# Longformer attention with a split-weight FFN: the first batch planned without mutual exclusion of VectorE and GpSimd

## The chip, the core and the metric

One core of a Trainium2 chip runs the whole program. The metric is the device time of one execution in microseconds. Engines are named as in the profile: PE (TensorE), DVE (VectorE), ACT (ScalarE), POOL (GpSimd), SP (SyncE, which issues the DMA transfers here). Each engine runs its own instructions strictly in the order in which the program gives them; semaphores make one engine wait for another.

## What is computed

Eight batches of attention (8 heads, 512 local and 32 global positions, head size 64) are followed by a feed-forward network with a leaky ReLU of one slope per unit:

```python
mask = np.abs(pos[:, None] - pos[None, :]) <= 32
s_ll = np.where(mask, scale * q_l @ k_l.T, -1e9)
a_l = sm(np.concatenate([scale * q_l @ k_g.T, s_ll], axis=-1))
out_l = a_l @ np.concatenate([v_g, v_l])
out_g = sm(scale * q_g @ k_all.T) @ v_all
x = concat(out_g, out_l)              # 4608 x 512
h = x @ w_in                          # 512 -> 2048
g = np.maximum(h, 0) + alpha * np.minimum(h, 0)
y = g @ w_out                         # 2048 -> 512
```

The weights come as 64-bit floats and are decoded on the chip into two single-precision parts (an upper and a lower one); inputs of the two products are split in the same way, and three of the four partial products are added up.

## The kernel before

**Tiling.** A batch has four pairs of heads (P runs over all 32 pairs) and 16 blocks of 128 hidden units (t, or f within a batch). For each block PE forms h = x times w_in (12 matmuls, `f1`) into a PSUM bank, DVE and ACT make g from it, and PE adds g times w_out into four banks (8 matmuls `fa` with the upper part of g, 4 `fb` with the lower part `gl`). The attention of the next batch runs between these blocks.

**Batch 0 is different.** Before its first product there is attention of four pairs to do, and the weights have to be decoded while they are first used: 32 halves (k = 2f + j; j = 0 is w_in, j = 1 is w_out). One half takes the steps below. The names are those of the plan, with the number of the half behind them (d314 is d3 of half 14).

| step | engine | what |
|---|---|---|
| Lw | SP | load the raw words |
| cv, ab | ACT | low words to integers, absolute value of the high ones |
| d1, d2, d3 | DVE | clamp, shift (both TENSOR_SCALAR, wraw from wraw), sign (SCALAR_TENSOR_TENSOR, wt from wraw) |
| ia | POOL | add the rounding (TENSOR_TENSOR, wt from wt and wr) |
| ca | ACT | upper part |
| su | DVE | lower part (TENSOR_TENSOR, wt from wt) |

Other names that the prediction uses: S, T, V, G are PE's scores, transposes, value products and global scores of a pair; red, mn, rza, rzr are DVE's row maximum, its negation, the sum and its reciprocal, nm POOL's normalisation that rzr releases; gm, gz are the statistics of the global rows and gsc their normalisation (POOL for the first four pairs); tq, tr are DVE transposes; xl are lower parts of x; be makes beta from alpha; p makes g from PSUM, gh (ACT) and gl (DVE) are its two parts; yl are the lower parts of the x of batch 1 (yl0 to yl3, one for each pair).

**What sets the order.** The order in batch 0 is not that of loops. `early` lists some 690 operations with engine, cost in microseconds and needs; `Plan.run` schedules them: each engine has a time at which it is free, an operation can start when its needs are done, and among those that can start about now the one that is due first (`due_times`, shifted by a bias for each kind from the table `LIST`) is taken. The operations are issued in the order that comes out, and the engines of batch 0 keep it. In the version before, operations marked `lock=True` (nm and gsc of POOL, d1, d2, d3, su, yl and gl of DVE, ia of POOL and the making of the mask) never overlapped in the plan: `lock` is the time at which the last of them ended, and the next may not start earlier.

```python
if o["lock"]:
    t = max(t, lock)
...
free[e] = stop = t + cost
if o["lock"]:
    lock = stop
```

That holds in the plan only. On the chip nothing in the program keeps DVE and POOL apart; only the order in which their instructions stand was made with it.

**Behind batch 0.** From t = 16 on the order comes from loops: `slow_unit` for batch 1, whose DVE, ACT and POOL instructions a scheduler of the language may place earlier or later (PE's stay), and `fast_unit` from batch 2 on, which saves matmuls with sums of x and of weights. `weight_sums` (wsum on DVE, 8 groups of six operations) prepares these in batch 1.

Of the kernel before, what the change touches and what calls it, by code (L numbers as in the profile page):

```python
# [37 lines left out]
GOFF = 1024  # L38
GROWS = {1: (0, 0), 4: (0, 1), 7: (0, 2), 10: (1, 0), 13: (1, 1), 15: (1, 2)}
LIST = dict(  # L40
    first=29.416, pace=6.054, pair0=79.515, pair=19.51, slack=2, vsub=1, ahead=6, inflight=4, near=0.1, vgl=1, half=True,
    bias=dict(ab=14, rzr=20, red=-20, fb=10, mem=12, su=1, gm=-25, gsc=-3, rza=9, xA=-15, yh=-24, G=5, Tg=-8, yl=-8, pt=-6, n=2, Lw=16, Lv=-12, cv=5, al=15, T=-29, sr=-13, mk=-10, gz=-15, sq=-20, S=-4, fa=-6, V=4, fy=-15, gh=15, xg=-6, xlA=-15, hr=17, mn=-1, Lq=-1, tr=-2, f=-6, p=-1, gexp=-5, tq=-3, xlB=-1, clear=6, be=2, fx=3),
)
FAST = range(2 * NF, NB * NF)
CATCH = (16, 23, 30)
# [15 lines left out]
class Plan:  # L61
# [3 lines left out]
        self.slots = {k: [0.0] * n for k, n in slots.items()}  # L65
        self.ops, self.slack, self.near, self.bias = {}, slack, near, bias

    def op(self, name, engine, cost, needs=(), lock=False, take=(), free=(), kind=None, due=None, n=1):
        assert name not in self.ops, name
        self.ops[name] = dict(engine=engine, cost=cost, needs=[x for x in needs if x], lock=lock, take=take, free=free, kind=kind, due=due, n=n)  # L70

    def due_times(self):
        users = {n: [] for n in self.ops}
# [23 lines left out]
    def run(self):  # L97
        ops, users = self.ops, self.due_times()
        end, order = {}, []
        free = dict(PE=5.4, ACT=2.5, DVE=5.0, POOL=4.0, SP=1.2)  # L100
        lock, dma, kind, landed = 0.0, 3.3, None, [0.0] * 8
        left = {n: len(o["needs"]) for n, o in ops.items()}
        ready = {n for n, k in left.items() if k == 0}
        while ready:
            can = []
            for n in sorted(ready):
                o = ops[n]
                e = o["engine"]
                if any(len(self.slots[p]) < k for p, k in o["take"]):
                    continue  # L110
                t = free[e]
                for x in o["needs"]:
                    y = ops[x]["engine"]
                    lag = -100.0 if y == e == "SP" and n[0] != "h" else 0.3 if y == "PE" else 0.12
                    t = max(t, end[x] + lag)
                for p, k in o["take"]:
                    t = max(t, sorted(self.slots[p])[k - 1])
                if o["lock"]:
                    t = max(t, lock)
                if e == "SP":  # L120
                    t = max(t, landed[o["n"] - 9])
                can.append((t, o["at"], n))
            assert can, sorted(ready)
            t, _, n = min(can)
            e = ops[n]["engine"]
            t, _, n = min((c for c in can if ops[c[2]]["engine"] == e and c[0] <= t + self.near), key=lambda c: (c[1], c[0]))
            o = ops[n]
            cost = o["cost"]
            if e == "PE":
                cost = cost * (1.25 if t < 45 else 1.03) + (0.15 if kind != o["kind"] else 0.0)  # L130
                kind = o["kind"]
            if e == "SP":
# [24 lines left out]

def early(first, pace, pair0, pair, slack, vsub, ahead, inflight, near, vgl=0, half=False, bias={}):

    plan = Plan({"st": NST - 2, "w": NWB}, slack, near, bias)  # L160
    op = plan.op

    for P in range(9):
        pre = P < NRAW
# [6 lines left out]
        due = pair0 + pair * (P - 5) if P > 4 else None  # L171
# [11 lines left out]
        for h in range(2):  # L183
            old = [f"nm{P-2}.{e}" for e in range(2)] if P > 1 else []
            if not pre and h == 0:
                old.append(f"sq{P-1}" if P > NRAW else f"T{P-2}")
            op(f"red{P}.{h}", "DVE", 0.61 if pre else 0.86, [f"S{P}", f"red{P}.0" if h else None, None if pre else "mk0"] + old)
            if pre:
                op(f"mn{P}.{h}", "DVE", 0.07, [f"red{P}.{h}"])
            hold = h == 0 and pre  # L190
            op(f"ex{P}.{h}", "ACT", 1.5, [f"mn{P}.{h}" if pre else f"red{P}.{h}", f"ex{P}.0" if h else None, f"T{P-2}" if hold and P > 1 else None], take=(("w", 1),) if hold and P % 2 else ())
            op(f"rza{P}.{h}", "DVE" if pre else "ACT", 0.08 if pre else 0.13, [f"ex{P}.{h}"])
            op(f"rzr{P}.{h}", "DVE", 0.1, [f"rza{P}.{h}"])
            op(f"nm{P}.{h}", "POOL", 1.0, [f"rzr{P}.{h}"], lock=True)
# [6 lines left out]
        op(f"gexp{P}", "ACT", 0.52, [f"gm{P}", f"Tg{P-1}" if P else None])  # L201
        op(f"gz{P}", "DVE", 0.55, [f"gexp{P}"])
        if pre:
            op(f"gsc{P}", "POOL", 0.8, [f"gz{P}"], lock=True)
        else:
            op(f"gsc{P}", "ACT", 0.53, [f"gz{P}"])
        last = first + pace * 15.5 if P == 8 else None
        if not pre:
            op(f"tq{P}", "DVE", 1.23, [f"nm{P}.0", f"nm{P}.1"], due=last)
# [28 lines left out]
        if not pre:  # L238
            c = P - NPAIR
            op(f"yh{c}", "ACT", 0.53, [f"xA{P}", f"xB{P}"], take=(("st", 2),), due=first + pace * 15)  # L240
            op(f"yl{c}", "DVE", 0.61, [f"yh{c}"], lock=True, due=first + pace * 15.5)
    op("clear", "POOL", 0.18, [f"Tg{NGP-1}"])
    op("mk0", "POOL", 0.6, ["Tg0"], lock=True)
    op("al0", "SP", 0.3, ["Lq0"])
    op("be0", "DVE", 0.1, ["al0"])
    for P in (9, 10):
# [1 line left out]
    for k in range(2 * NF):  # L248
        f, j = divmod(k, 2)
        op(f"Lw{k}", "SP", 1.31, [f"d3{k-ahead}" if k >= ahead else None], take=(("w", 1),))  # L250
        op(f"cv{k}", "ACT", 0.66, [f"Lw{k}", f"su{k-inflight}" if k >= inflight else None], take=(("st", 1),))
        op(f"ab{k}", "ACT", 0.58, [f"cv{k}"])
        op(f"d1{k}", "DVE", 0.33, [f"ab{k}"], lock=True)
        op(f"d2{k}", "DVE", 0.34, [f"d1{k}"], lock=True)
        op(f"d3{k}", "DVE", 0.61, [f"d2{k}"], lock=True, take=(("st", 1),), free=(("w", 1),))
        op(f"ia{k}", "POOL", 1.25, [f"d3{k}"], lock=True, free=(("st", 1),))
        op(f"ca{k}", "ACT", 0.54, [f"ia{k}"], take=(("w", 1),))
        slow = not (vsub and k % vsub == vsub - 1)
        op(f"su{k}", "POOL" if slow else "DVE", 1.25 if slow else 0.61, [f"ca{k}"], lock=True, free=(("st", 1),))
    for t in range(NF):  # L260
        x = [f"xl{a}{P}" for P in range(NPAIR) for a in "AB"]
        if t < 2:
            op(f"fx{t}", "PE", 1.41, [f"su{2*t}", "xg1"] + x[:4] + ([f"fx{t-1}"] if t else []), kind="f", due=first + pace * t - 4)
            op(f"fy{t}", "PE", 0.71, [f"fx{t}"] + x[4:6], kind="f", due=first + pace * t - 2)
        op(f"f1{t}", "PE", 0.71 if t < 2 else 2.82, ([f"fy{t}"] if t < 2 else [f"su{2*t}", f"p{t-2}"]) + x + ([f"f1{t-1}"] if t else []), kind="f", due=first + pace * t)
        if half:
            op(f"n{t}", "ACT", 0.54, [f"f1{t}"], take=(("st", 1),))
            op(f"p{t}", "DVE", 0.62, [f"n{t}", "be0"])
        else:
            op(f"p{t}", "DVE", 1.38, [f"f1{t}", "al0"], take=(("st", 1),))  # L270
        gslow = not (vgl and t % vgl == vgl - 1)
# [947 lines left out]
```

## Time and profile before

| | |
|---|---|
| time, median of 3 runs | 901.49 us (897.94, 901.49, 902.32) |
| the profiled execution, time | 897.03 us |
| its span, first to last instruction | 895.3 us |
| instructions | 22474 |
| mean granted clock of PE | 0.994 |
| DMA | 201 MB, mean 225 GB/s |

The span is what the trace covers; the time has about 1.7 us more around it. Times in the trace count from the start of the span. "Busy" is the share in which an engine had an instruction of its own running; an instruction that has started and is held up counts as busy, so a longer duration can hide a wait. PEld is the loading of weights into PE, which overlaps its matmuls. Rows of the timeline give start, duration, engine, line of the code (L293 is the helper through which DVE, ACT, POOL and SP instructions are issued, L322 the one for matmuls, so one goes by the tiles), operation, output and inputs, shapes and a count, and in brackets the idle time of the engine before it with what ended it. Consecutive instructions of one engine overlap by about 0.08 us in these rows.

### The profile page before, as it was taken

Reading aid. Unit: us, or ns where it says so; the run is one execution under the profiler, and the core shown is the slowest. Engines: PE = TensorE matmul, PEld = TensorE weight load, DVE = VectorE, ACT = ScalarE, POOL = GpSimd, SP = SyncE. Lnnn points to the kernel's source line nnn. Section 1 sums busy time; section 2 is a strip of 40 time slices with the busy share of each in tenths; the row PEclk is TensorE's granted clock in tenths of the full one; section 3 lists DMA queues with packets and bytes.
Section 4 is the critical chain, followed back from the end, with each engine's and each line's share of the span. In section 5 each row is a group of like instructions: output and inputs, shape, how many; then the busy total and the mean of one; then the engine's idle time right before and its main releaser. Section 6 shows DMA issues by size and latency. Waiting matters only on the chain.

```text
span 895.3 us, 22474 instructions
## 1 busy us (share of the span) xinstructions
PE 872.0 (97%) x8678; PEld 753.5 (84%) x8678; DVE 625.0 (70%) x1704; ACT 385.4 (43%) x1150; POOL 320.3 (36%) x279
## 2 busy tenths in 40 slices
PE   7899999999999999999999999999999999999997
PEld 5677777878888888888888888888889898998897
DVE  7999999976876667766776667756776657445532
ACT  6898885444354334433244334433344322211211
POOL 4545443654443332332333333332332322222221
PEclk9999999999999999999999999999999999999999
DMA  9879998967458666766657666766767533655530
GB/s 361 332 255 375 340 331 251 333 237 228 143 177 285 195 221 215 261 222 236 227 172 263 198 209 214 261 230 222 229 205 242 176 133 101 206 170 197 197 120 25
DMA packets 80906, 201.23 MB, mean 225 GB/s; under 512 B 21280, under 2 KB 41248, under 8 KB 77088
## 3 DMA queue, kind: packets, MB, share of 16 engines
q1 hardware_dynamic: 80800, 199.80, 65.4%
q8 instruction: 69, 1.13, 0.5%
q14 instruction: 37, 0.30, 0.1%
HBM read 160.96 MB, written 38.80 MB: 223 GB/s over the span
## 4 chain that ended last, share of the span: by engine, by line
PE 68%; DVE 18%; ACT 6%; DMA 5%; issue 2%; SPq 1%; POOL 0%; DVEq 0%; ACTq 0%
PE o L322 31%; PE h_ps L322 27%; DVE g L293 4%; PE o_ps L322 4%; PE s_ps L322 3%; ACT p L293 3%; DVE wt L293 2%; DVE wsum L293 2%; DVE xl L293 2%; PE g_ps L322 2%; DVE p L293 2%; DMA scratch<-p 2%; DVE wraw L293 1%; DMA qk<-in_qk_dram 1%; DMA pt<-scratch 1%
## 5 line engine op out<-in xcount | busy, mean ns | idle before, releaser
L293 POOL TENSOR_TENSOR gl<-g,gh 128x512 fp32r<-128x512 f32 (+1 forms) x128 | 159.3, 1244 | 376.7 <-ACT gh L293 304.8
L322 PE MATMUL o<-gh,wo 128*128 128x512 f32 (+1 forms) x1024 | 243.9, 381 | 0.0
L322 PE MATMUL h_ps<-xh,wt 128*128 128x256 f32 (+1 forms) x1120 | 240.4, 309 | 2.7 <-DVE wt L293 1.1
L293 ACT CAST gh<-g 128x512 fp32r<-128x512 f32 (+1 forms) x144 | 85.9, 597 | 306.1 <-DVE g L293 301.2
L322 PEld LDWEIGHTS o<-gh,wo 128*128 128x128 f32 x1024 | 176.7, 188 | 31.8 <-issue 0.4
L322 PEld LDWEIGHTS h_ps<-xh,wt 128*128 128x128 f32 x1120 | 181.9, 189 | 22.7 <-issue 4.4
L322 PE MATMUL h_ps<-xl,wt 128*128 128x256 f32 (+1 forms) x560 | 171.6, 306 | 0.8 <-DVE xl L293 0.8
L322 PE MATMUL o<-gl,wo 128*128 128x512 f32 (+1 forms) x512 | 130.9, 378 | 0.0
L293 DVE TENSOR_SCALAR g<-h_ps,alpha_sb 128x512 f32<-128x512 f32 (+1 forms) x128 | 91.6, 716 | 37.2 <-PE h_ps L322 31.2
L322 PEld LDWEIGHTS h_ps<-xl,wt 128*128 128x128 f32 x560 | 106.1, 189 | 6.4 <-DVE xl L293 1.0
L322 PE MATMUL h_ps<-xh,s 128*128 128x256 f32 x576 | 105.6, 280 | 3.3 <-DVE h_ps L293 2.0
L322 PEld LDWEIGHTS o<-gl,wo 128*128 128x128 f32 x512 | 92.7, 188 | 18.3
L293 POOL TENSOR_TENSOR p<-p,rz 128x512 f32<-128x512 f32 x64 | 71.9, 1138 | 97.2 <-DVE rz L293 92.1
L322 PEld LDWEIGHTS h_ps<-xh,s 128*128 128x128 f32 x576 | 90.9, 188 | 8.7 <-issue 4.5
L293 DVE TENSOR_TENSOR h_ps<-u,h_ps 128x256 f32<-128x256 f32 x144 | 61.1, 424 | 50.6 <-PE h_ps L322 49.0
L293 ACT ACTIVATE p<-p,mn 128x128 f32<-128x128 f32 x224 | 86.9, 395 | 3.4 <-DVE mn L293 2.9
L293 DVE SCALAR_TENSOR_TENSOR g<-h_ps,g 128x512 f32<-128x512 f32 (+1 forms) x128 | 84.1, 657 | 4.1
L293 DVE TENSOR_TENSOR u<-u,h_ps 128x256 f32<-128x256 f32 x96 | 40.3, 420 | 61.8 <-PE h_ps L322 38.6
L322 PE MATMUL h_ps<-xl,s 128*128 128x256 f32 x288 | 80.9, 281 | 1.4 <-DVE xl L293 0.9
L293 POOL TENSOR_TENSOR wt<-wt,wr 128x512 int32<-128x512 int32 x32 | 45.4, 1423 | 52.4 <-DVE wt L293 35.3
L322 PEld LDWEIGHTS o_ps<-pt,v 128*64 128x64 f32 x1600 | 50.3, 139 | 7.8 <-issue 3.1
L322 PEld LDWEIGHTS h_ps<-xl,s 128*128 128x128 f32 x288 | 54.2, 188 | 2.6 <-DVE xl L293 2.6
(95 smaller groups left out, 1057.7 us busy)
## 6 DMA issues: line engine op xcount, KB each, us to landing
wo<-wo SPq DMA_DIRECT2D x128, 512.0 KB, 4.2
v<-in_v_dram SPq DMA_DIRECT2D x29, 1024.0 KB, 5.8
qk<-in_qk_dram SPq DMA_DIRECT2D x30, 672.0 KB, 7.0
wraw<-in_w_dram SPq DMA_DIRECT2D x32, 512.0 KB, 8.1
scratch<-p SPq DMA_DIRECT2D x112, 128.0 KB, 2.8
pt<-scratch SPq DMA_DIRECT2D x28, 512.0 KB, 5.5
wo<-wt SPq DMA_DIRECT2D x16, 512.0 KB, 7.5
out_dram<-ost SPq DMA_DIRECT2D x32, 256.0 KB, 3.4
```

The lines of the kernel that those rows point to most:

```text
L293: ins = op(*a, **k)
L322: ins = nc.tensor.matmul(*a, **k)
```

## The change

`Plan` loses the lock: the argument, the wait and the update go, and DVE's and POOL's operations may overlap in the plan. Some costs are set anew: POOL's ia from 1.25 to 1.4, su and gl on POOL from 1.25 to 1.45 (none is put on POOL with this table), nm from 1.0 to 1.05 for the first four pairs and 1.25 for the others, ex 1.5 to 1.54; PE's operations are counted 1.25 times their cost up to 27 us instead of 45, and 1.0 instead of 1.03 times behind it; the engines are free some 0.5 to 0.9 us earlier at the start. Then the table `LIST` (first product's due time, pace, biases) is another one. The same operations run on the same engines with the same operands; only the order on each engine changes, in batch 0 and, where the scheduler of the language fills in, in the first blocks of batch 1. No buffer, semaphore or computation is altered.

```diff
 LIST = dict(
-    first=29.416, pace=6.054, pair0=79.515, pair=19.51, slack=2, vsub=1, ahead=6, inflight=4, near=0.1, vgl=1, half=True,
+    first=26.474, pace=6.175, pair0=70.132, pair=19.51, slack=2, vsub=1, ahead=6, inflight=4, near=0.1, vgl=1, half=True,
...
     def run(self):
         ops, users = self.ops, self.due_times()
         end, order = {}, []
-        free = dict(PE=5.4, ACT=2.5, DVE=5.0, POOL=4.0, SP=1.2)
-        lock, dma, kind, landed = 0.0, 3.3, None, [0.0] * 8
+        free = dict(PE=4.5, ACT=2.5, DVE=4.2, POOL=3.2, SP=0.7)
+        dma, kind, landed = 2.4, None, [0.0] * 8
...
-                if o["lock"]:
-                    t = max(t, lock)
...
-                cost = cost * (1.25 if t < 45 else 1.03) + (0.15 if kind != o["kind"] else 0.0)
+                cost = cost * (1.25 if t < 27 else 1.0) + (0.12 if kind != o["kind"] else 0.0)
...
-                if o["lock"]:
-                    lock = stop
...
-        op(f"d3{k}", "DVE", 0.61, [f"d2{k}"], lock=True, take=(("st", 1),), free=(("w", 1),))
-        op(f"ia{k}", "POOL", 1.25, [f"d3{k}"], lock=True, free=(("st", 1),))
+        op(f"d3{k}", "DVE", 0.61, [f"d2{k}"], take=(("st", 1),), free=(("w", 1),))
+        op(f"ia{k}", "POOL", 1.4, [f"d3{k}"], free=(("st", 1),))
```

Three places of the new order matter here. The line numbers of the changed kernel are four smaller, and the numbers of tiles differ between the two programs.

The first is on DVE in the middle of batch 0, behind the signs d315 and d316, each of which releases an add (ia) on POOL. Before, from d315 on (p7, the two halves of the transpose tq6, d118, su16, d218, gl6, d318, d117, xg5):

```order
L293 SCALAR_TENSOR_TENSOR wt_1514<-wraw_1215 128x512
L293 SCALAR_TENSOR_TENSOR g_1516<-g_1516,beta_sb_70,h_ps_1421 128x512
L293 STREAM_TRANSPOSE p_1415<-p_1415 128x512 x2
L293 TENSOR_SCALAR wraw_1270<-wraw_1270 128x512
L293 TENSOR_TENSOR wt_1474<-wt_1441,wt_1474 128x512
L293 TENSOR_SCALAR wraw_1270<-wraw_1270 128x512
L293 TENSOR_TENSOR gl_1410<-g_1343,gh_1409 128x512
L293 SCALAR_TENSOR_TENSOR wt_1565<-wraw_1270 128x512
L293 TENSOR_SCALAR wraw_1294<-wraw_1294 128x512
L293 COPY x_glb_74<-o_ps_1477 128x32
```

The changed order there (d316, d115, d118, d215, gl6, su13, d315, su16, d218, d117, d318):

```order
L289 SCALAR_TENSOR_TENSOR wt_1377<-wraw_1109 128x512
L289 TENSOR_SCALAR wraw_1120<-wraw_1120 128x512
L289 TENSOR_SCALAR wraw_1183<-wraw_1183 128x512
L289 TENSOR_SCALAR wraw_1120<-wraw_1120 128x512
L289 TENSOR_TENSOR gl_1419<-g_1360,gh_1418 128x512
L289 TENSOR_TENSOR wt_1424<-wt_1351,wt_1424 128x512
L289 SCALAR_TENSOR_TENSOR wt_1438<-wraw_1120 128x512
L289 TENSOR_TENSOR wt_1435<-wt_1377,wt_1435 128x512
L289 TENSOR_SCALAR wraw_1183<-wraw_1183 128x512
L289 TENSOR_SCALAR wraw_1208<-wraw_1208 128x512
L289 SCALAR_TENSOR_TENSOR wt_1464<-wraw_1183 128x512
```

The slopes and the transposes that stood behind a sign have gone elsewhere; decode operations follow one another, with a sign every five or six of them.

The second is on DVE at the end of batch 0. Before, behind su30 (yl1, yl2, yl3, d229, d231, d329, d331, gz8, p14):

```order
L293 TENSOR_TENSOR wt_2222<-wt_2176,wt_2222 128x512
L293 TENSOR_TENSOR xl_1554<-x_raw_73,xh_1553 128x512
L293 TENSOR_TENSOR xl_1872<-x_raw_73,xh_1871 128x512
L293 TENSOR_TENSOR xl_2210<-x_raw_73,xh_2209 128x512
L293 TENSOR_SCALAR wraw_1945<-wraw_1945 128x512
L293 TENSOR_SCALAR wraw_2032<-wraw_2032 128x512
L293 SCALAR_TENSOR_TENSOR wt_2256<-wraw_1945 128x512
L293 SCALAR_TENSOR_TENSOR wt_2258<-wraw_2032 128x512
L293 TENSOR_SCALAR gz_2192<-gz_2192 64x1 x2
L293 RECIPROCAL gz_2192<-gz_2192 128x1
L293 SCALAR_TENSOR_TENSOR g_2234<-g_2234,beta_sb_70,h_ps_2196 128x512
```

The changed order behind p13 (d331, su29, gl13, rzr8.1, su31, a first weight sum, p14, tq8, more of the sum, gl14):

```order
L289 SCALAR_TENSOR_TENSOR g_2136<-g_2136,beta_sb_70,h_ps_2084 128x512
L289 SCALAR_TENSOR_TENSOR wt_2163<-wraw_1917 128x512
L289 TENSOR_TENSOR wt_2139<-wt_2112,wt_2139 128x512
L289 TENSOR_TENSOR gl_2168<-g_2136,gh_2167 128x512
L289 RECIPROCAL rz_2131<-rz_2131 128x4
L289 TENSOR_TENSOR wt_2172<-wt_2163,wt_2172 128x512
L289 TENSOR_TENSOR wsum_2544<-wt_626 128x512
L289 TENSOR_TENSOR wsum_2544<-wt_715 128x512
L289 SCALAR_TENSOR_TENSOR g_2209<-g_2209,beta_sb_70,h_ps_2150 128x512
L289 STREAM_TRANSPOSE p_2102<-p_2102 128x512 x2
L289 TENSOR_TENSOR wsum_2544<-wsum_2544 128x256
L289 TENSOR_TENSOR gl_2216<-g_2209,gh_2215 128x512
```

Decoding now ends earlier in the order, the value product of the last pair (V7 on PE) and with it the fourth lower part yl3 stand later, and two groups of weight sums of batch 1 are filled in ahead of p15; yl3 comes four operations behind the last row.

The third is the start of SP's queue. Before, alpha is the last of these (its 10th to 18th transfer):

```order
L293 DMA wraw_206<-in_w_dram 128x1024
L293 DMA v_256<-in_v_dram 128x1024
L293 DMA v_257<-in_v_dram 128x1024
L293 DMA v_276<-in_v_dram 128x1024
L293 DMA v_277<-in_v_dram 128x1024
L293 DMA wraw_291<-in_w_dram 128x1024
L293 DMA wraw_365<-in_w_dram 128x1024
L293 DMA qk_384<-in_qk_dram 128x1344
L293 DMA alpha_sb_69<-in_alpha_dram 128x16
```

The changed queue (its 5th to 12th transfer):

```order
L289 DMA v_152<-in_v_dram 128x2048
L289 DMA q_154<-in_qk_dram 128x576
L289 DMA k_155<-in_qk_dram 128x768
L289 DMA wraw_158<-in_w_dram 128x1024
L289 DMA wraw_162<-in_w_dram 128x1024
L289 DMA alpha_sb_69<-in_alpha_dram 128x16
L289 DMA v_255<-in_v_dram 128x1024
L289 DMA v_256<-in_v_dram 128x1024
```

Alpha is issued as the 10th transfer; on DVE its reader be0 moves from behind d31 to just behind mn2.1, ahead of d10.

More of the change, by code (lines that the diff above doesn't have):

```diff
@@ L40 @@
 LIST = dict(
-    first=29.416, pace=6.054, pair0=79.515, pair=19.51, slack=2, vsub=1, ahead=6, inflight=4, near=0.1, vgl=1, half=True,
-    bias=dict(ab=14, rzr=20, red=-20, fb=10, mem=12, su=1, gm=-25, gsc=-3, rza=9, xA=-15, yh=-24, G=5, Tg=-8, yl=-8, pt=-6, n=2, Lw=16, Lv=-12, cv=5, al=15, T=-29, sr=-13, mk=-10, gz=-15, sq=-20, S=-4, fa=-6, V=4, fy=-15, gh=15, xg=-6, xlA=-15, hr=17, mn=-1, Lq=-1, tr=-2, f=-6, p=-1, gexp=-5, tq=-3, xlB=-1, clear=6, be=2, fx=3),
+    first=26.474, pace=6.175, pair0=70.132, pair=19.51, slack=2, vsub=1, ahead=6, inflight=4, near=0.1, vgl=1, half=True,
+    bias=dict(ab=15, red=-20, fb=7, mem=12, gm=-13, gsc=-3, rza=9, xA=-14, yh=-24, gl=12, G=5, Tg=-9, n=2, Lw=4, Lv=3, cv=5, al=15, T=-29, sr=-12, gz=-15, S=-4, fa=-5, V=4, gh=15, xg=-12, xlA=-3, hr=17, mn=-4, Lq=-1, tr=-2, f=-6, gexp=-5, tq=-9, xlB=-1, be=20, ia=-10, su=1, ptg=-5, rzr=-1, pt=-15, sq=-20, mk=1),
 )
@@ L66, in __init__, with op @@
         self.ops, self.slack, self.near, self.bias = {}, slack, near, bias
-    def op(self, name, engine, cost, needs=(), lock=False, take=(), free=(), kind=None, due=None, n=1):
+    def op(self, name, engine, cost, needs=(), take=(), free=(), kind=None, due=None, n=1):
         assert name not in self.ops, name
-        self.ops[name] = dict(engine=engine, cost=cost, needs=[x for x in needs if x], lock=lock, take=take, free=free, kind=kind, due=due, n=n)
+        self.ops[name] = dict(engine=engine, cost=cost, needs=[x for x in needs if x], take=take, free=free, kind=kind, due=due, n=n)
     def due_times(self):
@@ L190, in early @@
             hold = h == 0 and pre
-            op(f"ex{P}.{h}", "ACT", 1.5, [f"mn{P}.{h}" if pre else f"red{P}.{h}", f"ex{P}.0" if h else None, f"T{P-2}" if hold and P > 1 else None], take=(("w", 1),) if hold and P % 2 else ())
+            op(f"ex{P}.{h}", "ACT", 1.54, [f"mn{P}.{h}" if pre else f"red{P}.{h}", f"ex{P}.0" if h else None, f"T{P-2}" if hold and P > 1 else None], take=(("w", 1),) if hold and P % 2 else ())
             op(f"rza{P}.{h}", "DVE" if pre else "ACT", 0.08 if pre else 0.13, [f"ex{P}.{h}"])
             op(f"rzr{P}.{h}", "DVE", 0.1, [f"rza{P}.{h}"])
-            op(f"nm{P}.{h}", "POOL", 1.0, [f"rzr{P}.{h}"], lock=True)
+            op(f"nm{P}.{h}", "POOL", 1.05 if pre else 1.25, [f"rzr{P}.{h}"])
         if P <= NRAW:
@@ L203, in early @@
         if pre:
-            op(f"gsc{P}", "POOL", 0.8, [f"gz{P}"], lock=True)
+            op(f"gsc{P}", "POOL", 0.8, [f"gz{P}"])
         else:
-            op(f"gsc{P}", "ACT", 0.53, [f"gz{P}"])
+            op(f"gsc{P}", "ACT", 0.56, [f"gz{P}"])
         last = first + pace * 15.5 if P == 8 else None
@@ L240, in early @@
             op(f"yh{c}", "ACT", 0.53, [f"xA{P}", f"xB{P}"], take=(("st", 2),), due=first + pace * 15)
-            op(f"yl{c}", "DVE", 0.61, [f"yh{c}"], lock=True, due=first + pace * 15.5)
+            op(f"yl{c}", "DVE", 0.61, [f"yh{c}"], due=first + pace * 15.5)
     op("clear", "POOL", 0.18, [f"Tg{NGP-1}"])
-    op("mk0", "POOL", 0.6, ["Tg0"], lock=True)
+    op("mk0", "POOL", 0.6, ["Tg0"])
     op("al0", "SP", 0.3, ["Lq0"])
@@ L252, in early @@
         op(f"ab{k}", "ACT", 0.58, [f"cv{k}"])
-        op(f"d1{k}", "DVE", 0.33, [f"ab{k}"], lock=True)
-        op(f"d2{k}", "DVE", 0.34, [f"d1{k}"], lock=True)
-        op(f"d3{k}", "DVE", 0.61, [f"d2{k}"], lock=True, take=(("st", 1),), free=(("w", 1),))
-        op(f"ia{k}", "POOL", 1.25, [f"d3{k}"], lock=True, free=(("st", 1),))
+        op(f"d1{k}", "DVE", 0.33, [f"ab{k}"])
+        op(f"d2{k}", "DVE", 0.34, [f"d1{k}"])
+        op(f"d3{k}", "DVE", 0.61, [f"d2{k}"], take=(("st", 1),), free=(("w", 1),))
+        op(f"ia{k}", "POOL", 1.4, [f"d3{k}"], free=(("st", 1),))
         op(f"ca{k}", "ACT", 0.54, [f"ia{k}"], take=(("w", 1),))
         slow = not (vsub and k % vsub == vsub - 1)
-        op(f"su{k}", "POOL" if slow else "DVE", 1.25 if slow else 0.61, [f"ca{k}"], lock=True, free=(("st", 1),))
+        op(f"su{k}", "POOL" if slow else "DVE", 1.45 if slow else 0.61, [f"ca{k}"], free=(("st", 1),))
     for t in range(NF):
@@ L272, in early @@
         op(f"gh{t}", "ACT", 0.54, [f"p{t}"], take=(("st", 2),))
-        op(f"gl{t}", "POOL" if gslow else "DVE", 1.25 if gslow else 0.61, [f"gh{t}"], lock=True, free=(("st", 1),))
+        op(f"gl{t}", "POOL" if gslow else "DVE", 1.45 if gslow else 0.61, [f"gh{t}"], free=(("st", 1),))
         if t >= NF - LAG:
```

## The prediction, made before the changed kernel was run

> **What bounds the kernel now.** I read the page's busy shares first, then the stages, then the chain of work that ended last.
>
> ```profile
> PE 872.0 (97%) x8678; PEld 753.5 (84%) x8678; DVE 625.0 (70%) x1704; ACT 385.4 (43%) x1150; POOL 320.3 (36%) x279
> ```
>
> PE is full on average, but the change reorders batch 0 and a few operations behind it, so the stages count. Columns: stretch in us, its length, then busy time of PE, PEld, DVE, ACT, POOL, the granted PE clock, DMA share, GB/s.
>
> ```profile
> 7.20:20.00 12.80, 9.86 (x247) 6.62 (x249) 11.31 (x38) 11.17 (x56) 6.41 (x7) 1.00 1.03 405
> 20.00:48.50 28.50, 23.92 (x379) 19.33 (x376) 27.46 (x92) 24.27 (x68) 14.07 (x13) 0.88 0.84 326
> 48.50:144.00 95.50, 93.11 (x868) 73.46 (x867) 93.19 (x246) 81.56 (x210) 47.77 (x35) 1.00 0.89 318
> 152.70:200.00 47.30, 46.95 (x437) 37.91 (x437) 41.17 (x105) 21.52 (x70) 27.50 (x23) 1.00 0.84 293
> 200.00:895.00 695.00, 684.23 (x6594) 606.37 (x6592) 441.37 (x1195) 242.09 (x742) 219.18 (x185) 1.00 0.60 199
> ```
>
> Batch 0 ends near 148 us. Up to 144, DVE is idle 1.5 + 1.0 + 2.3 = 4.8 us only; PE is idle 2.9 + 4.6 + 2.4 us. Behind 152.7 PE has no slack (0.35 us of 47.3, 11 of 695), so what batch 0 gains or loses stays in the total. The chain of work that ended last agrees: from 27 to some 175 us it runs mostly on DVE.
>
> ```profile
> 27.20 0.64 DVE wraw L293
> ...
> 175.79 1.79 DVE wsum L293
> ```
>
> So the question is how long DVE needs for the operations of batch 0. They are the same 270 before and after; only their neighbours change.
>
> **The term that decides: DVE and GpSimd do exclude each other.** Rows of the timeline: start, duration, engine, operation.
>
> ```profile
> 77.33 0.68 DVE L293 SCALAR_TENSOR_TENSOR wt<-wraw 128x512 uint32<-128x512 uint32 x1
> 77.93 0.42 DVE L293 TENSOR_SCALAR wraw<-wraw 128x512 f32<-128x512 f32 x1
> 78.27 1.78 DVE L293 TENSOR_TENSOR wt<-wt 128x512 fp32r<-128x512 f32 x1
> 78.18 1.32 POOL L293 TENSOR_TENSOR wt<-wt,wr 128x512 int32<-128x512 int32 x1 [1.85 <-ACT wt L293]
> 87.07 1.26 DVE L293 TENSOR_SCALAR wraw<-wraw 128x512 uint32<-128x512 uint32 x1
> 86.56 1.48 POOL L293 TENSOR_TENSOR p<-p,rz 128x512 f32<-128x512 f32 x1
> 112.20 1.45 DVE L293 TENSOR_TENSOR wt<-wt 128x512 fp32r<-128x512 f32 x1
> 111.96 1.13 POOL L293 TENSOR_TENSOR p<-p,rz 128x512 f32<-128x512 f32 x1 [0.72 <-DVE rz L293]
> 67.38 1.13 DVE L293 TENSOR_TENSOR wt<-wt 128x512 fp32r<-128x512 f32 x1
> ```
>
> The subtraction su11 starts at 78.27 and ends at 80.05, 0.55 us behind the end of GpSimd's add (79.50): it stood until the add was done. Unhindered its kind takes 0.68 us, d1/d2 0.42, d3 0.68. The losses are 1.10 (78.27), 0.84 (87.07), 0.77 (112.20) and 0.45 us (67.38). They are inside busy time: no idle shows. What is not held:
>
> ```profile
> 89.36 0.75 DVE L293 SCALAR_TENSOR_TENSOR g<-g,beta_sb,h_ps 128x512 f32<-128x512 f32 x1 [0.29 <-ACT g L293]
> 90.02 1.30 DVE L293 STREAM_TRANSPOSE p<-p 128x512 f32<-128x512 f32 x2
> 88.56 1.41 POOL L293 TENSOR_TENSOR p<-p,rz 128x512 f32<-128x512 f32 x1 [0.51 <-DVE rz L293]
> 89.93 1.28 POOL L293 TENSOR_TENSOR wt<-wt,wr 128x512 int32<-128x512 int32 x1
> 91.24 0.39 DVE L293 TENSOR_SCALAR wraw<-wraw 128x512 f32<-128x512 f32 x1
> ```
>
> p, which reads PSUM, and the transposes run at full speed under GpSimd's operations; the next d1 comes at 91.24, when the add has ended, and loses nothing. So d1, d2, d3, su, gl, yl and the small statistics lose time when they stand within about 1.25 us behind an operation that starts GpSimd; reductions, p and transposes are free filler. The groups by form give the sum for 20 to 152.7 us (count, busy us, mean ns):
>
> ```profile
> L293 DVE TENSOR_TENSOR wt<-wt 128x512 fp32r<-128x512 f32 x32 | 25.5, 798 | 0.1
> L293 DVE SCALAR_TENSOR_TENSOR wt<-wraw 128x512 uint32<-128x512 uint32 x32 | 22.9, 725 | 0.0
> L293 DVE TENSOR_SCALAR wraw<-wraw 128x512 f32<-128x512 f32 x32 | 15.3, 485 | 0.0
> L293 DVE TENSOR_SCALAR wraw<-wraw 128x512 uint32<-128x512 uint32 x32 | 15.1, 476 | 0.0
> ...
> L293 POOL TENSOR_TENSOR wt<-wt,wr 128x512 int32<-128x512 int32 x32 | 45.4, 1423 | 52.4 <-DVE wt L293 35.3 <-ACT wraw L293 6.1 <-ACT p L293 4.1
> ```
>
> Over 0.68, 0.68, 0.42 and 0.42 us apiece that is 3.7 + 1.1 + 1.9 + 1.7 = 8.4 us. So d3 is held as well (0.725 for 0.68). With the small statistics of the first 35 us (one that waited and one that did not stand below) and one gl, I count some 23 waits and about 12 us.
>
> ```profile
> 10.76 0.60 DVE L293 TENSOR_SCALAR mn<-mn 128x4 f32<-128x4 f32 x1
> ...
> 16.36 0.17 DVE L293 TENSOR_SCALAR mn<-mn 128x4 f32<-128x4 f32 x1
> ```
>
> GpSimd's mean of 1.42 us for an add is the other half of the same thing: it waits too when DVE got in first. The change takes that mean for the add's own length and drops the exclusion.
>
> **Part 1, more collisions.** I went through DVE's order before and after with one rule: GpSimd starts 0.2 us behind the DVE operation that releases it; if the next DVE operation is of the held kinds it goes first; the next held one then waits until 1.25 (ia), 1.04 (nm) or 0.8 us (gsc) have passed, less the free filler between. Before: 4 waits of a whole operation (1.0 us or more), 15 of 0.3 to 1.0 and 7 small ones, 15 us; the trace has 12. After: 19 whole ones and 24 of 0.3 to 1.0, 39 us. In the first piece of order shown above, d315 was followed by p, a transpose and then d1; now su and d2 follow at once. Price of a whole wait by the rows: 0.45 (where two GpSimd operations stood back to back) to 1.10; I take 0.95, since most of the 19 are built like 78.27. Of a partial one: (12 - 3.2) / 19 = 0.46, so 0.5. After: 19 x 0.95 + 24 x 0.5 = 30 us, between 20 (19 x 0.45 + 24 x 0.46) and 39. Against 12: **+18 us, bounds +8 and +27**. Nothing hides it: DVE runs in order and is idle for 4.8 us in all.
>
> **Part 2, DVE's idle time.** A later DVE finds its inputs ready. Of the 4.8 us I take 3 as gone: **-3, bounds 0 and -4.8**. GpSimd stays far from full (47.8 of 95.5 us), ACT at 81.6 of 95.5 is looser when DVE is slower.
>
> **Part 3, the end of the batch.** Behind p13 stand, in the new order, d3, su, gl, su, two weight sums, p14, the transposes, another sum, gl14, one more sum, and then the fourth xl (yl3), which PE needs for the last quarter of its first product of batch 1. Before, the four xl stood ahead and no sum did. PE's rows there (f115, fb13, and the first product of batch 1), and the sums by form (152.7 to 200 us):
>
> ```profile
> 144.05 0.62 PE L322 MATMUL h_ps<-xh,wt 128*128 128x512 f32 x2
> 146.80 1.08 PE L322 MATMUL o<-gl,wt 128*128 128x512 f32 x4
> 148.42 0.74 PE L322 MATMUL h_ps<-xh,wt 128*128 128x512 f32 x2 [0.53 <-DVE g L293]
> L293 DVE TENSOR_TENSOR wsum<-wsum 128x256 f32<-128x256 f32 x20 | 13.7, 684 | 0.4
> L293 DVE TENSOR_TENSOR wsum<-wt 128x512 f32<-128x512 f32 x10 | 9.2, 963 | 0.0
> ```
>
> From f115's start PE has 2.75 (f115) + 1.0 (fb13) + 2.1 us (three quarters) = 6 us before it needs yl3. DVE has 4 x 0.6 + 0.9 of waiting + 2 x 0.96 + 2 x 0.68 + p 0.66 + 1.2 + gl 0.6 + xl 0.6 = 9.6 us. That is 3.5 us of waiting, and p15, behind another 7 sums, is late for the bank of the second product by some 2.5 more: **+6, bounds 0 and +9**. The sums are then off DVE's list later, where PE waited for nothing, so nothing comes back.
>
> **Part 4, the start.** SP now issues alpha as its 10th transfer instead of its 18th, near the place of these (the 9th and 10th of before), whose kind took so long to land (min/median/max):
>
> ```profile
> 5.13 1.74 SPq L293 DMA_DIRECT2D wraw<-in_w_dram  x2
> DMA to landing us min/median/max: 7.2/10.8/13.0
> ```
>
> So alpha lands at 13 to 20 us. Its reader be0 moves up to just behind mn2.1, which ran at 16.4 us (the 16.36 row) and now has a copy and gm1 ahead of it: I take 0, at most +2.
>
> **Sum.** 18 - 3 + 6 = **+21 us**, on the profiled execution's 897.0: 918. Its time is the lowest of four (897.9, 901.5 and 902.3 are the runs, median 4.5 above it); their mean is 899.7, so I forecast 920.5.
>
> **A rule of the Trainium skill, in sentences apart.** Its page "SBUF — State Buffer", section "SBUF: two separate sides", says that VectorE (in a two-port mode or with two SBUF inputs) and GpSimd share one port pair under an exclusive lock, and that the loser blocks for the whole instruction. That speaks against the change, and the 78.27 row agrees; the 67.38 row (0.45 us lost) is milder. By the rule at its full price the stalls are 39 us and the total 929.7 by my other terms.
>
> **Rivals.** (a) *TensorE's clock turns the pauses into more.*
>
> ```profile
> 20.90:24.40 3.50, 1.87 (x33) 1.29 (x27) 3.35 (x10) 3.50 (x18) 1.92 (x3) 1.00 1.03 421
> 24.40:27.80 3.40, 3.31 (x36) 2.99 (x36) 3.01 (x14) 2.35 (x7) 3.02 (x4) 0.50 1.03 403
> ```
>
> After a stretch with PE half idle the clock is 0.50 for 3.4 us, up to 1.7 us of work lost. New pauses are about 0.6 us per 3.4 us, too few for it unless they bunch; eight such drops give +13, 933. The Trainium skill ("TensorE: Matmul & The Clock Gate", Part 1) ties the drop to a whole idle window of about 3.4 us; by that rule the case would be out, but the 20.90 row dropped with 1.87 of 3.50 busy. (b) *The collisions fall where DVE would have waited anyway*, on ACT or PE: for it, the new order lets the first products start earlier; against it, 4.8 us of idle is all there is. Within 0.5% of now, 901. (c) *Faster*: the place is 7 to 48 us, where PE idles 7.5 us and runs at half clock twice (2 x 1.7); gsc0 and the first decode now go earlier. It decides only if collisions grow by less than these 10 us; with +5 of them: 895.
>
> **How the numbers follow.** Forecast 0.75, (a) 0.09, (b) 0.07, (c) 0.09. The bounds of parts 1 to 4 add up to +3 and +38 (903 to 938); ends that all fall together are rare, so the range is 905 to 936, which leaves out (b), (c) and the top of (a). Faster by over 0.5% (about what a measurement of this kernel can tell from no change) 0.09, within 0.07, slower 0.84.
>
> **What would show it.** Right: the means of wt<-wt, wt<-wraw and wraw<-wraw on DVE rise (in sum by 12 us or more over 8.4); PE idles for DVE's wt, g or xl by 12 us or more between 48 and 165 us; the last product of batch 0 starts near 159 instead of 144; behind 200 us nothing changes. Wrong: those means stay, or rise while DVE's idle time falls by as much, or a second product of batch 1 starts before 155.

## The result, and the profile after

| | before | after |
|---|---|---|
| time, median of 5 runs (lowest, highest) | 899.28 us (897.94, 902.32) | 926.88 us (923.19, 931.18) |
| ratio, 95% interval | | 1.0309 (1.0281 to 1.0337) |
| span of the profiled execution | 895.3 us | 925.3 us |

The changed kernel is slower by 27.6 us; 920.5 was forecast, in a range of 905 to 936. First the busy shares of the changed kernel, in the same form as those of the kernel before.

```profile
PE 883.7 (95%) x8676; PEld 762.4 (82%) x8678; DVE 640.9 (69%) x1704; ACT 386.2 (42%) x1150; POOL 324.6 (35%) x279
```

PE's and DVE's busy times rose by 11.7 and 15.9 us without one more operation. The stages (stretch and length in us; busy PE, PEld, DVE, ACT, POOL; granted clock; DMA share; GB/s) say where:

```profile
48.50:144.00 95.50, 83.14 (x672) 64.38 (x673) 91.29 (x211) 69.98 (x176) 45.58 (x29) 0.91 0.76 264
144.00:175.00 31.00, 23.37 (x209) 18.07 (x208) 30.05 (x66) 16.06 (x44) 12.26 (x10) 0.89 0.71 243
200.00:895.00 695.00, 688.92 (x6671) 605.70 (x6670) 450.27 (x1223) 247.63 (x763) 223.85 (x186) 1.00 0.62 206
```

From 48.5 to 144 DVE is as busy as before (91.3 against 93.2) but gets through 211 instructions instead of 246, and PE through 672 instead of 868, with 12.4 us idle. From 144 to 175 PE is idle for another 7.6. Behind 200 us PE is full, as before. The same decode operations as in the prediction, by form (count, busy us, mean ns):

```profile
L289 DVE TENSOR_TENSOR wt<-wt 128x512 fp32r<-128x512 f32 x32 | 31.5, 987 | 3.2 <-ACT wt L289 3.0
L289 DVE SCALAR_TENSOR_TENSOR wt<-wraw 128x512 uint32<-128x512 uint32 x32 | 23.4, 733 | 0.2
L289 DVE TENSOR_SCALAR wraw<-wraw 128x512 uint32<-128x512 uint32 x32 | 20.1, 631 | 0.2
L289 DVE TENSOR_SCALAR wraw<-wraw 128x512 f32<-128x512 f32 x32 | 19.2, 610 | 0.0
L289 POOL TENSOR_TENSOR wt<-wt,wr 128x512 int32<-128x512 int32 x32 | 52.5, 1647 | 64.7 <-DVE wt L289 29.6 <-ACT p L289 8.9 <-ACT wraw L289 7.3
```

Over their own lengths (0.68, 0.68, 0.42, 0.42) DVE's four come to 9.8 + 1.7 + 6.8 + 6.1 = 24.4 us of waiting, against 8.4 before. GpSimd's add went from 1.42 to 1.65 us apiece: it waits too.

For the comparisons below I counted every wait of DVE in batch 0 in the rows: what a held operation (d1, d2, d3, su, gl, yl, the small statistics, a weight sum over a whole tile) took beyond its own time, where that is over 0.15 us. Before it is 11.9 us (23 waits), after 31.8 (45). The times of the experiments beside it (medians; ratios to the kernel before, run alongside on the same chip):

| kernel | us | ratio (95% interval) | DVE's waits, us |
|---|---|---|---|
| after | 926.9 | 1.0309 (1.0281 to 1.0337) | 31.8 |
| 1 after, lock back | 921.4 | 1.0277 (1.0251 to 1.0303) | 25.5 |
| 2 before, lock off | 932.7 | 1.0398 (1.0374 to 1.0421) | 31.3 |
| 3 after, short add | 903.4 | 1.0068 (1.0049 to 1.0088) | 10.0 |
| 4 before, short add | 895.9 | 0.9988 (0.9971 to 1.0004) | 4.2 |
| 5 lock off, short add | 909.5 | 1.0128 (1.0107 to 1.0149) | 9.8 |
| 6 after, memset in the add | 908.4 | 1.0106 (1.0073 to 1.0140) | 14.0 |
| 7 after, sums kept back | 927.4 | 1.0324 (1.0302 to 1.0345) | 33.7 |
| 8 after, x of pair 7 first | 925.2 | 1.0302 (1.0280 to 1.0324) | 33.7 |
| 9 after, both | 927.7 | 1.0314 (1.0284 to 1.0344) | 32.2 |
| 10 after, both, short add | 902.3 | 1.0063 (1.0039 to 1.0088) | 8.3 |
| 11 lock, new costs, new table | 899.3 | 1.0012 (0.9991 to 1.0033) | 9.6 |
| 12 before, new table | 902.7 | 1.0039 (1.0023 to 1.0056) | 10.8 |

### The profile page after: what moved, and what is told of

It reads as the page before. It is cut to its first block, busy times and chain, and to the rows that moved or that the text cites. A ratio compares the mean times of both kernels' runs of the same rounds, so it can differ in the third digit from the quotient of the medians.

```text
span 925.3 us, 22474 instructions
## 1 busy us (share of the span) xinstructions
PE 883.7 (95%) x8676; PEld 762.4 (82%) x8678; DVE 640.9 (69%) x1704; ACT 386.2 (42%) x1150; POOL 324.6 (35%) x279
## 4 chain that ended last, share of the span: by engine, by line
PE 71%; DVE 21%; ACT 4%; issue 2%; POOL 1%; DMA 1%; SPq 0%; DVEq 0%; ACTq 0%; POOLq 0%
PE o L318 32%; PE h_ps L318 29%; DVE wt L289 4%; PE o_ps L318 4%; DVE g L289 3%; DVE wraw L289 3%; PE s_ps L318 3%; PE g_ps L318 2%; DVE xl L289 2%; ACT p L289 2%; DVE p L289 1%; DVE x_raw L289 1%; DVE wsum L289 1%; DVE gl L289 1%; DVE gm L289 1%
## 5 line engine op out<-in xcount | busy, mean ns | idle before, releaser
L318 PE MATMUL h_ps<-xh,wt 128*128 128x256 f32 (+1 forms) x1120 | 243.9, 311 | 6.0 <-DVE wt L289 3.6
L318 PEld LDWEIGHTS h_ps<-xh,wt 128*128 128x128 f32 x1120 | 183.8, 190 | 27.3 <-issue 5.6
L318 PEld LDWEIGHTS o<-gl,wo 128*128 128x128 f32 x512 | 92.8, 188 | 18.4
L289 POOL TENSOR_TENSOR wt<-wt,wr 128x512 int32<-128x512 int32 x32 | 52.5, 1647 | 64.7 <-DVE wt L289 29.6
L318 PE MATMUL o_ps<-pt,v 128*64 128x32 f32 (+1 forms) x1600 | 55.3, 228 | 8.8 <-issue 8.0
```

Source lines behind the costliest of these rows:

```text
L289: ins = op(*a, **k)
L318: ins = nc.tensor.matmul(*a, **k)
```

## The experiments

**1 and 2. Is it the lock in the plan?** One puts the lock back into the changed plan, the other takes it out of the plan of before.

```diff
 # 1, in the changed kernel (and lock=True at the operations that had it)
+                if o["lock"]:
+                    t = max(t, lock)
...
+                if o["lock"]:
+                    lock = stop
```

> The changed kernel with the lock put back into the plan, everything else of the change (costs, table) kept. Rule of the prediction applied to its order on VectorE: 21 whole and 16 partial waits, 36 us, against 41 (20 and 26) for the changed kernel and 17 (5 and 16) for the kernel before. Theory (VectorE and GpSimd exclude each other on the chip, and what counts is whether free work stands behind a release): putting the lock back does not bring the time back, since the plan then waits where it finds no free work; waits of about 26 us in the trace against 30, time 915 to 928. Rival (the lock in the plan is what keeps the engines apart): about 900. Rival (the costs and the table alone, collisions aside): as the changed kernel, 925 to 928.

```diff
 # 2, in the kernel before
-                if o["lock"]:
-                    t = max(t, lock)
...
-                if o["lock"]:
-                    lock = stop
```

> The kernel before with only the lock taken out of the plan; table and costs as before. The same rule counts 19 whole and 23 partial waits, 37.5 us. Theory: about 27 us of waits in the trace instead of 12, so the time is 910 to 920 (899 + 15, less what the order of the end of batch 0 does). Rival (the new table and costs, not the lock, make the loss): 897 to 903, with the mean of GpSimd's wt<-wt,wr near 1.42 us.

The lock alone does not bring the time back (921.4, with 25.5 us of waits where 26 were expected): the plan then waits where it finds no free work, and the chip does the same. Nor does the table of before alone, as experiment 2 shows. It takes the lock and a table searched under it to lay free work behind GpSimd's starts. Taking the lock away without a new table is worse than the change: the waits (31.3) are near the 27 expected, but the time is 932.7 instead of 910 to 920. This miss is taken up in 5.

**3 and 4. Take the exclusion away, leave the orders.** GpSimd's add works on 8 columns instead of 512; the rounding of the other 504 is left out.

```diff
-            pool.tensor_tensor(t.bitcast(I32), t.bitcast(I32), r, op=ALU.add)
+            pool.tensor_tensor(t.bitcast(I32)[:, 0:8], t.bitcast(I32)[:, 0:8], r[:, 0:8], op=ALU.add)
```

> The changed kernel with GpSimd's rounding add ia on 8 of its 512 columns; the rounding of the other 504 is left out. Orders and counts of instructions stay. Theory: most waits between VectorE and GpSimd go, 20 to 26 of the 30 us, and with them the time: 900 to 907; PE's waits at the end of batch 0 remain. Rival (the new order itself is the loss: value products, TensorE's clock, the end of batch 0): 918 to 927, hardly less.

> The kernel before with the same short add (8 of 512 columns, the rest of the rounding left out). Theory: 6 to 9 of its 12 us of waits go, 890 to 894, so that the two kernels with the short add differ by 8 to 14 us instead of 27.6. Rival (the order itself): the difference of the two stays at 24 to 28.

The stages of both, first the changed kernel with the short add, then the kernel before with it:

```profile
48.50:144.00 95.50, 88.44 (x844) 69.24 (x843) 93.22 (x247) 79.23 (x200) 26.26 (x36) 1.00 0.88 305
144.00:175.00 31.00, 29.79 (x237) 23.86 (x238) 23.80 (x66) 15.20 (x45) 13.47 (x12) 0.89 0.91 331
```

```profile
48.50:144.00 95.50, 94.21 (x873) 74.37 (x872) 89.26 (x250) 81.40 (x212) 22.01 (x35) 1.00 0.91 325
```

In the changed kernel DVE is again through 247 instructions in the stage and PE through 844. Its time is 5.8 us above the kernel before of the same runs, where the change cost 27.6: the short add is worth 21.8 us here, for 21.8 us of waits. In the kernel before it is worth 1.7 (its interval includes no change) for 7.7 us of waits, and its 895.9 us miss the 890 to 894 expected: once DVE's waits go there, PE has 1.3 us of slack left in the stage and sets the pace. So the two orders differ by 7.5 us without the long add (8 to 14 were expected), and 20 of the 27.6 us hang on it.

**5. What else is in experiment 2.** The same edit in the kernel with the lock off.

> The kernel before with the lock taken out of the plan alone, as in the second experiment (932.7 us, 35 more than before, where its 31 us of waits, 19 more than before, would explain 19), with GpSimd's rounding add on 8 of 512 columns, the rounding of the other 504 left out. It tells what the other 16 us are. If they follow from the exclusion too (first products late, TensorE pausing and at half clock for it): the time falls by 25 to 35, to 898 to 908. If they are the order's own: it falls by 15 to 22 only, to 911 to 918, with the first slope (p0) still late, behind 54 us. Rival (TensorE's clock alone): 926 to 933.

The answer lies between the two: the time falls by 23 us, for 21.5 us of waits, and 12 us above the kernel before remain, which are the order's own. The stretch up to 60 us shows both parts. PE's longest wait there with the lock off, and then with the short add:

```profile
PE h_ps L318 <- DVE g L289: 5.6, 1, 5.6
```

```profile
PE h_ps L318 <- DVE g L289: 3.3, 1, 3.3
```

The first slope (p0) starts at 58.7 us with the lock off, at 53.0 with the short add and at 47.2 before: of the 11.5 us that the first products are late, 5.7 go with the exclusion and 5.8 are the order's. So the lock in the plan had done a second thing for the table of before, which was made under it: without it the first products come late.

**6. Exclusion, or only a shorter chain?** The short add also takes 1.1 us out of each half's way from d3 to ca. So GpSimd's time is filled up with a memset, and the second piece of the add holds ca back until it is over.

```diff
-            pool.tensor_tensor(t.bitcast(I32), t.bitcast(I32), r, op=ALU.add)
+            ti = t.bitcast(I32)
+            pool.tensor_tensor(ti[:, 0:8], ti[:, 0:8], r[:, 0:8], op=ALU.add)
+            pool.memset(r[:, 8:512], 0)
+            pool.tensor_tensor(ti[:, 8:16], ti[:, 8:16], r[:, 0:8], op=ALU.add)
```

> The changed kernel with GpSimd's rounding add cut to two pieces of 8 columns and a memset of 504 columns between them (the rounding of the other 496 columns is left out): GpSimd is as long about a half as with the whole add (0.25 + 0.55 + 0.25 us and gaps, about 1.2), but most of that time it only writes. This separates the two things that the short add took away, the exclusion and the 1.1 us of GpSimd's time in each half's chain. If the chain's length was the loss: 918 to 928. If the exclusion was, and a memset excludes nobody: 902 to 909, and VectorE's operations run at their own length beside the memset. If the exclusion was, and a memset holds VectorE off as an add does: 918 to 930, with waits of VectorE that end with the memset or the second piece.

908.4 us: 18.4 of the 27.6 us come back, although a half occupies GpSimd for 0.38 + 0.55 + 0.38 = 1.3 us, as a whole add does. It is 9.2 us above the kernel before, experiment 3 was 5.8: these 3.3 us are all that the chain's length can have cost, and DVE's waits are 4.0 us longer here, which would cover them. Rows of this kernel (start, duration, engine, operation):

```profile
115.13 1.22 DVE L289 TENSOR_SCALAR wraw<-wraw 128x512 f32<-128x512 f32 x2
115.55 0.52 POOL L289 MEMSET wr<- 128x504 int32 x1
...
144.97 0.51 POOL L289 MEMSET wr<- 128x504 int32 x1
145.14 0.69 DVE L289 TENSOR_TENSOR gl<-g,gh 128x512 fp32r<-128x512 f32 x1 [0.17 <-ACT gh L289]
```

gl starts 0.17 us into a memset and runs at its own length, 0.69. Two operations d1 or d2 end at 116.35 instead of 115.9 (0.42 twice, overlapping by 0.08): the second ended 0.28 us after the memset, which was over at 116.07. It is so throughout: nine operations d1 or d2 of this trace end behind a memset, each by 0.28 or 0.29 us; four others had started 0.08 us ahead of one and ran at their own 0.42, and then the memset took 0.80 instead of 0.52. All eight su and gl that ran beside a memset took 0.65 to 0.69. So a memset lets operations with two inputs pass and holds d1 and d2 off; "excludes nobody" was wrong by half. The Trainium skill ("SBUF — State Buffer", section "SBUF: two separate sides") says that VectorE with two SBUF inputs contends only with a GpSimd instruction that reads SBUF, and in a two-port mode with any. Both pairs of rows agree with it, if d1 and d2 run in such a mode, which no row shows.

**7 to 10. The end of batch 0.** In the changed kernel PE stands longest in front of G8, the global scores of pair 8. Rows from S8, the scores of that pair, over the last decode operations to the first product of batch 1:

```profile
147.98 1.29 PE L318 MATMUL s_ps<-qk 64*32 64x128 f32 x64
...
163.96 2.13 DVE L289 TENSOR_TENSOR wsum<-wt 128x512 f32<-128x512 f32 x2
166.01 0.73 DVE L289 SCALAR_TENSOR_TENSOR g<-g,beta_sb,h_ps 128x512 f32<-128x512 f32 x1
166.78 0.62 ACT L289 CAST gh<-g 128x512 fp32r<-128x512 f32 x1 [2.97 <-DVE g L289]
167.31 0.47 ACT L289 COPY x_raw<-o_ps 128x384 f32<-128x384 f32 x1
168.00 1.22 PE L318 MATMUL g_ps<-qk 128*64 128x288 f32 x6 [5.57 <-ACT x_raw L289]
169.15 3.63 PE L318 MATMUL o<-gh,wt 128*128 128x512 f32 x8
...
176.28 0.62 PE L318 MATMUL h_ps<-xh,wt 128*128 128x512 f32 x2
```

G8 waits for ACT's copies of the last value product, which stand behind gh14, which waits for p14, which stands behind two weight sums. Each of the edits takes out one link, and the last two kernels have both:

```diff
 # 7: the first sums stay behind batch 0's operations
+            pin[0] = t < NF + 6
             weight_sums((t - NF - 2) // 2)
+            pin[0] = False
 # 8: ACT's copies of pair 7 ahead of gh14
-        for name in plan.run():
+        order = plan.run()
+        for name in ("xA7", "xB7"):
+            order.remove(name)
+            order.insert(order.index("gh14"), name)
+        for name in order:
             issue(name)
```

> The changed kernel with the first three groups of weight sums kept behind batch 0 on VectorE (held in program order). Theory A, read from the trace of the changed kernel: TensorE stands 5.6 us before the global scores of pair 8 (G8), because G8 waits for the copy of x_raw on ScalarE, which stands behind gh14, which waits for p14, which stands behind two sums of 2.05 us; without them 2 to 3 us come back, 923 to 925.5. Theory B (step 3 of the prediction: the fourth lower part and p15 late behind the sums): 6 us come back, 919 to 922. Rival C (the sums are needed early by batch 2 and only move): 926 to 929.

> The changed kernel with ScalarE's two copies of the last value product (xA7, xB7) issued ahead of gh14 instead of behind it. Theory A: G8 starts near 162.5 instead of 168.0, and fa13 and f115 behind it as much earlier: 919.5 to 922.5. Theory B (yl3 and p15 decide): 925 to 928, since VectorE's order is the same. Rival D (VectorE has no room at all, so PE waits elsewhere): 925 to 928 too, with another wait of PE in place of the 5.6 us.

> Both of these edits: the sums behind batch 0 and the copies of pair 7 ahead of gh14. Theory A: the two gains overlap in one chain; 917 to 921, so 6 to 10 us of the 27.6 are the end of batch 0. Theory B: as with the sums alone.

> Both of these edits and GpSimd's rounding add on 8 of 512 columns (the rounding of the other 504 is left out). The changed kernel with the short add alone took 903.4, the kernel before with it 895.9: 7.5 us are left between the two orders. If these are the end of batch 0, this one takes 895 to 899; if they are elsewhere (the first products, TensorE's clock), 901 to 904.

The place gains, the total does not. The totals of the first three miss what this reading of the trace gave (923 to 925.5, 919.5 to 922.5 and 917 to 921), and that of the last, 902.3, lies where it was expected if the 7.5 us between the two orders are not the end of batch 0. PE's order is the same in all of them, so a stretch can be compared: from S8 to the first product of batch 1 it takes 28.3 us in the changed kernel (147.98 to 176.28), 25.8 with the sums kept back, 22.7 with the copies first and 22.7 with both; with the short add 24.4, and with both edits besides 19.0. Rows of G8, fa13 and the first product of batch 1 with the copies first, and behind them PE's largest wait later on:

```profile
166.90 0.70 PE L318 MATMUL g_ps<-qk 128*64 128x288 f32 x6 [1.97 <-ACT x_raw L289]
167.53 2.13 PE L318 MATMUL o<-gh,wt 128*128 128x512 f32 x8
173.16 0.62 PE L318 MATMUL h_ps<-xh,wt 128*128 128x512 f32 x2
```

```profile
PE o_ps L318 <- DMA pt<-scratch: 2.5, 1, 2.5
```

The 5.6 us are there, and then PE comes to the next value product before the transfer of its transposed scores has landed. With the sums kept back, they stand in the way a little later: ahead of gm, whose result ACT needs for the sg_sb that PE then waits for. With both edits and the short add:

```profile
202.77 1.14 PE L318 MATMUL s_ps<-qk 64*32 64x128 f32 x62 [3.13 <-ACT sg_sb L289]
203.84 3.68 PE L318 MATMUL o<-gh,wo 128*128 128x512 f32 x8
```

3.1 us of waiting, as in the two others with the sums kept back, and a product that takes 3.7 us instead of 2.1. The rest of the gain goes ahead of S8: though every engine has the same order up to there, S8 comes 1.3 (sums back), 2.5 (copies first) and 4.8 us (both) later in these single executions than in the changed kernel, so differences of this size ahead of S8 are scatter of one execution. In the medians, 925.2 to 927.7, none of the three gains what its place does. That the end of batch 0 holds some 5 us is shown by its stretch; that they can be had, or are part of the 7.5 us, was not found.

**11 and 12. A better order?** Two tables, picked by replaying many orders in a model that has the exclusion in it (no time here is from it): one for the changed kernel's costs with the lock back, one for the kernel before. Only `LIST` differs from experiment 1 and from the kernel before; of each the first numbers:

```diff
 # 11
-    first=26.474, pace=6.175, pair0=70.132, pair=19.51, slack=2,
+    first=-9.479, pace=6.048, pair0=63.986, pair=16.839, slack=2,
 # 12
-    first=29.416, pace=6.054, pair0=79.515, pair=19.51, slack=2,
+    first=-67.681, pace=5.53, pair0=91.115, pair=21.035, slack=2,
```

> The lock back in the plan with the new costs, and a table chosen anew for it, so that fewer held operations of VectorE stand behind a release of GpSimd: by the rule 2 whole and 16 partial waits, 13 us, against 17 (5 and 16) of the kernel before and 41 of the changed one. Theory: the time follows the waits, so it is close to the kernel before, 890 to 903; it can hardly gain more than 5 us, since TensorE is busy for 93 of 95.5 us between 48 and 144. Rival (the new costs or TensorE's order do harm): over 908.

> The kernel before (lock and costs as they were) with another table: 5 whole and 12 partial waits by the rule, 14 us against 17. Theory: 891 to 903, no clear difference to the kernel before. Rival (the time hangs on something else in the table than the waits): over 908.

With 9.6 and 10.8 us of waits the first is where the kernel before is and the second 0.4% above it. The first shows that the new costs do no harm: with the lock and a table made for it the loss is gone. Neither beats the kernel before, as experiment 4 would have it: fewer waits have little left to gain there.

## Why the prediction was right, and where not

**The mechanism** was right. The short add takes 20 us of the difference away without touching an order, and the memset keeps most of that gain while GpSimd is as busy as before.

**Part 1, +18 (8 to 27)**: DVE's waits grew by 19.9 us, of which the four decode operations alone make 16; experiments 3 and 4 put 20 us on the exclusion, what DVE idles for it included. The count of 39 us by rule was rightly cut to 30 (31.8). What the prediction did not see is that a microsecond of waiting has not the same price in both orders: the short add takes 21.8 us of waits away after and 7.7 before, 14.1 more, and this is worth 20.1 us, because the 7.7 were worth 1.7 only. That the term comes so near is in part luck.

**Part 2, -3 (0 to -4.8)** failed. DVE's idle time behind 20 us did not fall, it rose from 4.0 (to 152 us) to 7.2 (to 175). The step took a later DVE to find its inputs ready and left out that GpSimd loses in the exclusion as well. Rows of the changed kernel:

```profile
92.08 1.12 DVE L289 TENSOR_SCALAR wraw<-wraw 128x512 f32<-128x512 f32 x3
92.36 5.05 POOL L289 TENSOR_TENSOR wt<-wt,wr 128x512 int32<-128x512 int32 x2 [2.36 <-ACT gh L289]
93.09 0.71 DVE L289 TENSOR_TENSOR gl<-g,gh 128x512 fp32r<-128x512 f32 x1
93.69 0.71 DVE L289 TENSOR_TENSOR wt<-wt 128x512 fp32r<-128x512 f32 x1
94.29 0.71 DVE L289 SCALAR_TENSOR_TENSOR wt<-wraw 128x512 uint32<-128x512 uint32 x1
96.84 1.12 DVE L289 TENSOR_TENSOR wt<-wt 128x512 fp32r<-128x512 f32 x1 [1.84 <-ACT wt L289]
```

Six held operations of DVE follow one another without a gap up to 95.0; GpSimd's two adds, which start at 92.36, take 5.05 us instead of 2.5, and then DVE stands 1.84 us for the upper part (ca) that waits for the first of them. The same happens at 66.9 us, behind three adds that take 7.1 us. Together the two are nearly the whole rise; this line has no counterpart in the kernel before:

```profile
DVE wt L289 <- ACT wt L289: 3.0, 2, 1.8
```

The decode chain goes round through GpSimd, so its loss comes back to DVE.

**Part 3, +6 (0 to +9)**: the wait was another, and that the size fits is luck. PE stood 5.6 us, but for G8 behind ACT's copies, not for yl3 and the bank of p15. The sums that the prediction blamed are 2.5 us of it, the order on ACT the rest. TensorE also ran G8 and fa13 in 1.22 and 3.63 us, against 0.70 and 2.13 in experiment 8, 2.0 us more. But no edit of this place shortened the time by its size, so that it costs the total 6 us is not shown.

**Part 4, 0**: right; p0 starts at 48.2 us, 1.0 later than before.

**The sum**: 20 + 7.5 = 27.6 instead of 18 + (6 - 3) = 21. Of the 6.6 us short, 2 are in part 1 and 4.5 in what the order costs without the long add, for which the forecast had 6 - 3. The gain of 3 did not come; where these 7.5 us stand is open, since experiment 10 took the wait at the end of batch 0 away and got back 1.1.

**Rivals.** (b) and (c) are out: nothing was hidden, and the front end did not gain. (a), with a chance of 0.09, did happen in part: the clock of 0.91 and 0.89 in the two stages stands for (0.09 x 95.5 + 0.11 x 31) x 2 = 24 us at half clock, seven stretches, near the eight that were priced at +13. In experiment 3 five of the seven are gone, so they follow from the pauses that the exclusion makes. Their own price was not separated, apart from the 2.0 us of part 3; PE's busy time rose by 11.7 us, and 24 us at half clock can account for 12 at most. The time stayed below the 933 of this rival. It asked for pauses that bunch, and the traces say how much. In the fourteen profiles the stretches at full clock are made of windows of 3.41 us. Up to 880 us, all 44 windows with PE busy for less than 46% were followed by half clock, 14 of the 40 between 46 and 57%, and none of the others. PE need not be idle for a whole window.

**The signs.** The means rose by 16 us (12 or more wanted). PE idles for 20 us between 48.5 and 175, but this view names DVE's wt and g for 5.4 us only, where 12 were wanted:

```profile
PE o_ps L318 <- issue: 8.0, 3, 4.2
PE g_ps L318 <- ACT x_raw L289: 5.6, 1, 5.6
PE h_ps L318 <- DVE wt L289: 3.6, 3, 2.7
PE h_ps L318 <- DVE g L289: 1.8, 1, 1.8
```

The 5.6 stand behind DVE as shown, and the 8.0 are value products that start some 0.1 us behind the last score reduction of the next pair on DVE, which frees a bank. The longest of them:

```profile
133.06 0.08 DVE L289 DVE_READ_ACCUMULATOR2_ANT mn<- 128x1 f32 x1
133.24 0.59 PE L318 MATMUL o_ps<-pt,v 128*64 128x32 f32 x6 [4.21 <-issue]
```

That DVE releases them is read from the times only. f115 starts at 172.6 instead of the 159 forecast, because the new order of PE has V7 and G8 between f114 and f115, where the order of before had them ahead of f114: the wait that was booked behind f115 came before it. Behind 200 us nothing changed, as forecast.

## What to carry to other kernels

Two engines that exclude each other need an order that lays other work behind each start of the second one; a lock in a planner that only accounts for the waiting does not make such an order, a table searched under that lock did. A wait is worth its full price only on the engine that sets the pace at that place: the same short add was worth 21.8 us in one order and 1.7 in the other. And when a wait at one place is taken out, look at what is late next before counting it.

## What the runs showed that was not expected

A memset of 504 columns on GpSimd (0.51 us) holds TENSOR_SCALAR operations of VectorE off and lets those with two inputs run beside it. GpSimd loses against a full queue of VectorE: an add on 8 columns, 0.25 us alone, stood for 3.04 us while six held operations of DVE (between 62.0 and 64.6 us) went by, and showed as busy. Rows of experiment 6, where the same add later ran alone:

```profile
61.66 3.04 POOL L289 TENSOR_TENSOR wt<-wt,wr 128x8 int32<-128x8 int32 x1 [5.80 <-ACT wraw L289]
...
84.37 0.25 POOL L289 TENSOR_TENSOR wt<-wt,wr 128x8 int32<-128x8 int32 x1 [6.38 <-ACT sg_sb L289]
```

Who looks only for idle time does not see such a wait; the length of the same operation elsewhere shows it.
